# Delta-rule attention and two FFN layers: attention products with fp32 operands in place of f16 triples, and the first layer's output with tokens on rows

## The chip, the cores and the metric

The kernel runs on one core of a Trainium2 chip. The time is that of the device, in microseconds (us): the median of 3 runs, and one more execution under the profiler, which gives the trace. The engines of the core are TensorE (PE in the rows; its weight loads are PEld), VectorE (DVE), ScalarE (ACT), GpSimd (POOL) and SyncE (SP, whose queue issues nearly all DMAs).

## The reference

Attention over 4 batches, 8 heads, 768 positions and 48 features a head, then two FFN layers over all 3072 tokens:

```
for t in range(S):                       # state: 48 x 48 for each of 32 batch-heads, kept in fp32
    y[t] = q[t] @ state
    state = state + beta[t] * outer(kn[t], v[t] - kn[t] @ state)    # kn = k / (|k| + 1e-6)
x = y, as 3072 tokens x 384 features
x = leaky(x @ w1_in) @ w1_out            # 384 -> 2048 -> 384, leaky(h) = max(0.01 h, h)
x = g(x @ w2_in) @ w2_out                # 384 -> 2048 -> 384, g(h) = h - tanh(h)
```

## The kernel before

**Attention.** The sequence is cut into 12 chunks n of 64 positions; two chunks make a unit u. Within a chunk the recurrence is written with matrices: the Gram matrix of the keys (`grams`), the inverse of a unit triangular matrix (`inverses` solves its 32x32 blocks on VectorE; `merges` joins them with fp32 products of 32x32), the products of queries and keys under a causal mask (`products`), the update of the state (`states`) and the outputs (`outputs`). For every chunk there are 32 batch-heads, and a product of one head takes a quarter of TensorE's array, so four heads lie side by side. `t_batch` turns the keys: by DMA (`turn`) for chunks from 2 on, on TensorE for chunks 0 and 1.

**Numbers.** Except in `merges` and in the weights' folding, every operand is two f16 parts, a high one and the rest, and `heads` issues three products for one: high with high, high with low, low with high. VectorE and ScalarE make the parts. For queries, values and the layers' inputs they also measure a sum of squares, add it up over partitions with a product with `ones`, and scale by a power of two (`norm_sum`, `pow2_scale`, tiles `p`, `qs`, `sc`). Names in the rows: `KN` are the normalized keys in two parts, `KTp` the turned ones, `pq` queries or masked products, `XF` and `XH` the inverse (the rest and the high part), `R` the values, `S` the state and `SP` its parts.

**The FFN layers.** The tokens go in 12 tiles of 256, one for each chunk, through both layers. A layer has 8 pairs p of 128 hidden rows each way: `h_part` makes two times 9 products of 128x256 (`ps_h`), ScalarE and VectorE evict and activate (`g`, in two parts), and `o_part`, three pairs later, adds to the output (`ps_o`). Before the change the first layer holds its output with features on rows (18 products of 128x256 for a pair, `wo` stationary), the second with tokens on rows (12 products of 128x384, `g` stationary). `to_xb` evicts the first layer's output, measures it, splits it, and so makes the second layer's input.

**Weights.** `weight` builds the fp32 weights from their stored words on VectorE (rows `wi<-wo`, `wo<-wi`, 128x768 int32), then splits them: the high part on ScalarE, the rest on VectorE (`wo<-wo,sw,sx`). All of it must be done for a layer before its products start.

**The order.** `Graph` records every instruction; `schedule` places them by its own costs, by `tails` and by a table of numbers for each stage (`BIAS`), and `issue` writes them out in that order, engine by engine. All matrix products stand in the rows with line L607 (L609 after the change), and all other work with L610 (L612).

Of the kernel before, what the change touches and what calls it, by code (L numbers as in the profile page):

```python
# [30 lines left out]
def layers(n):  # L31
# [11 lines left out]
HI_DMA = ()  # L43
GQ = range(4)
# [4 lines left out]
SROOMS = 6  # L49
TURNS = 2  # L50
# [14 lines left out]
    ('dma', 'o_part1', 9): 53.93, ('dma', 'products', 1): -84.66, ('dma', 'products', 10): 73.75,  # L65
    ('dma', 'products', 11): 11.76, ('dma', 'products', 2): 87.05, ('dma', 'products', 3): -36.92,
    ('dma', 'products', 4): 60.79, ('dma', 'products', 5): 6.28, ('dma', 'products', 6): 120.47,
    ('dma', 'products', 7): 1.76, ('dma', 'products', 8): 8.32, ('dma', 'products', 9): -13.13,
    ('dma', 'queries', 0): 263.24, ('dma', 'queries', 1): 49.48, ('dma', 'queries', 10): 237.19,
    ('dma', 'queries', 11): -96.51, ('dma', 'queries', 2): -18.27, ('dma', 'queries', 3): -1.42,  # L70
    ('dma', 'queries', 4): 103.52, ('dma', 'queries', 5): 32.48, ('dma', 'queries', 6): 168.36,
    ('dma', 'queries', 7): 48.61, ('dma', 'queries', 8): 188.4, ('dma', 'queries', 9): 95.39,
    ('dma', 'to_xa', 1, 1): 43.27, ('dma', 'to_xa', 10, 1): 6.08, ('dma', 'to_xa', 11, 1): -4.4,
    ('dma', 'to_xa', 2, 1): 158.76, ('dma', 'to_xa', 3, 1): -109.25, ('dma', 'to_xa', 4, 1): 26.99,
    ('dma', 'to_xa', 5, 1): 100.67, ('dma', 'to_xa', 6, 1): 195.78, ('dma', 'to_xa', 8, 1): 20.17,
    ('dma', 'to_xa', 9, 1): 106.46, ('dma', 'v', 0): 375.3, ('dma', 'weight', 0, 0): 152.98,
    ('dma', 'weight', 0, 1): -16.73, ('dma', 'weight', 0, 2): -9.76, ('dma', 'weight', 0, 3): -81.63,
    ('dma', 'weight', 0, 4): -175.79, ('dma', 'weight', 0, 5): 3.96, ('dma', 'weight', 1, 0): 143.66,
    ('dma', 'weight', 1, 1): 108.98, ('dma', 'weight', 1, 2): 4.7, ('dma', 'weight', 1, 3): 80.95,
    ('dma', 'weight', 1, 4): 338.49, ('dma', 'weight', 1, 5): -33.2, ('dma', 'weight', 2, 0): 14.3,  # L80
    ('dma', 'weight', 2, 1): 238.2, ('dma', 'weight', 2, 2): 32.45, ('dma', 'weight', 2, 3): 11.3,
    ('dma', 'weight', 2, 4): 31.05, ('dma', 'weight', 2, 5): 94.83, ('dma', 'weight', 3, 0): 248.49,
    ('dma', 'weight', 3, 1): 141.54, ('dma', 'weight', 3, 2): -0.74, ('dma', 'weight', 3, 3): -101.97,
    ('dma', 'weight', 3, 4): 9.37, ('dma', 'weight', 3, 5): -192.26, ('first_keys', 0): 36.95,
    ('grams', 0): 41.82, ('grams', 0, 1): 47.41, ('grams', 1): 22.14, ('grams', 1, 1): 545.82,
    ('grams', 10, 1): -67.64, ('grams', 11, 1): -45.82, ('grams', 2, 1): -6.45, ('grams', 3, 1): 86.29,
    ('grams', 4, 1): -4.81, ('grams', 5, 1): -55.27, ('grams', 6, 1): 294.71, ('grams', 7, 1): -2.74,
# [6 lines left out]
    ('inverses', 0, 1): 7.54, ('inverses', 1): -33.65, ('inverses', 1, 1): 9.63, ('inverses', 2): 247.78,  # L94
    ('inverses', 2, 1): -291.34, ('inverses', 3): 28.99, ('inverses', 3, 1): -90.95, ('inverses', 4): -11.47,
    ('inverses', 4, 1): 407.53, ('inverses', 5): -6.42, ('inverses', 5, 1): 24.22, ('keys', 10): -70.46,
    ('keys', 11): 42.88, ('keys', 2): 2.73, ('keys', 3): -32.66, ('keys', 4): -249.54, ('keys', 5): -149.34,
    ('keys', 6): -33.29, ('keys', 7): -264.06, ('keys', 8): -28.32, ('keys', 9): -3.58, ('merges', 0): 61.65,
    ('merges', 0, 0): 236.37, ('merges', 0, 1): -4.82, ('merges', 1): 53.87, ('merges', 1, 1): -498.51,
    ('merges', 2): 1.17, ('merges', 2, 0): -95.98, ('merges', 2, 1): 8.62, ('merges', 3): 95.77,  # L100
    ('merges', 3, 0): -13.72, ('merges', 3, 1): -0.04, ('merges', 4): 1.69, ('merges', 4, 0): 64.24,
    ('merges', 4, 1): -40.43, ('merges', 5): -13.87, ('merges', 5, 0): -39.61, ('merges', 5, 1): 144.74,
# [124 lines left out]
class Graph:  # L227
# [116 lines left out]
    def matmul(self, o, lhsT, rhs, start, stop):  # L344
# [1201 lines left out]
```

## Time and profile before

| | |
|---|---|
| median of 3 runs | 978.83 us (977.82 to 979.18) |
| profiled execution | 976.78 us, its span 975.1 us |
| TensorE busy | 888.6 us (91%) |
| VectorE busy | 701.7 us (72%) |
| ScalarE busy | 582.0 us (60%) |
| moved by DMA | 67.01 MB, 69 GB/s mean |

The span is the time from the first to the last instruction in the trace; 1.7 us of the profiled execution lie outside it. A busy share is a mean over stages: up to the first product of the FFN layers the engines stand differently to one another than after it.

### The profile page before, as it was taken

The page shows a single profiled execution, that of the slowest core. Times are in us where ns is not written, and L with a number is a line of the kernel's source. Part 1 is how long each engine was busy: PE and PEld are TensorE (multiplying, and loading weights), DVE is VectorE, ACT ScalarE, POOL GpSimd, SP SyncE. Part 2 cuts the span into 40 slices and gives each one's busy share as a digit, 9 for nine tenths or more (in the row PEclk, how much of TensorE's full clock was granted, in tenths as well). Part 3 has the DMA queues.
Part 4 walks back from the last instruction along what each step waited for, and adds up shares of the span by engine and source line. Part 5 has one row for each costly group of instructions (what it writes and reads, how often), then busy time and mean ns, then how long its engine had stood idle before and what let it go on. Part 6 is the DMA issues. An engine that isn't in the chain of part 4 may idle for free.

```text
span 975.1 us, 35824 instructions
## 1 busy us (share of the span) xinstructions
PE 888.6 (91%) x15960; PEld 722.7 (74%) x15960; DVE 701.7 (72%) x1664; ACT 582.0 (60%) x1327; POOL 6.3 (1%) x23
## 2 busy tenths in 40 slices
PE   1236499999999999999999999999999999999997
PEld 1113488876788887788887788877788877788875
DVE  7999999999699845699873993566628957332432
ACT  6596897667786855565853645654545465444432
POOL 2000000000000000000000000000000000000000
PEclk9998599999999999999999999999999999999999
DMA  9945645222424200141020410002200000010000
GB/s 348 396 156 151 158 132 170 88 66 50 98 84 88 47 2 18 34 101 48 8 40 8 91 38 2 24 25 56 52 17 17 9 19 20 19 33 1 2 17 17
DMA packets 69274, 67.01 MB, mean 69 GB/s; under 512 B 42752, under 2 KB 54016, under 8 KB 69120
## 3 DMA queue, kind: packets, MB, share of 16 engines
q1 hardware_dynamic: 69120, 64.74, 24.3%
q8 instruction: 124, 2.03, 0.9%
q14 instruction: 30, 0.25, 0.1%
HBM read 44.14 MB, written 4.72 MB: 50 GB/s over the span
## 4 chain that ended last, share of the span: by engine, by line
PE 77%; DVE 9%; DMA 6%; ACT 5%; issue 1%; SPq 0%; ACTq 0%; DVEq 0%
PE ps_h L607 36%; PE ps_o L607 35%; PE ps_a L607 7%; DMA wo<-in_w_in_dram 3%; ACT sx L610 2%; DMA wi<-in_w_out_dram 2%; DVE sx L610 1%; DVE pq L610 1%; DVE gd L610 1%; ACT jk L610 1%; DVE wi L610 1%; DMA vf<-in_v_dram 1%; DVE xi L610 1%; DVE R L610 1%; ACT wi L610 1%
## 5 line engine op out<-in xcount | busy, mean ns | idle before, releaser
L607 PE MATMUL ps_h<-x,wi 128*128 128x256 f16 x3456 | 406.6, 273 | 0.6 <-ACT sx L610 0.4
L607 PEld LDWEIGHTS <-wi 128*128 128x128 f16 x3456 | 334.1, 98 | 47.2 <-issue 1.2
L607 PE MATMUL ps_o<-g,wo 128*128 128x256 f16 x1728 | 203.8, 273 | 0.5 <-DVE g L610 0.5
L607 PE MATMUL ps_o<-wo,g 128*128 128x384 f16 x1152 | 201.2, 326 | 0.3 <-DVE g L610 0.3
L607 PEld LDWEIGHTS <-wo 128*128 128x128 f16 x1728 | 167.1, 98 | 20.3 <-issue 0.6
L610 ACT ACTIVATE g<-sx 128x512 f16<-128x512 f32 x192 | 120.0, 627 | 83.4 <-DVE sx L610 52.8
L607 PEld LDWEIGHTS <-g 128*128 128x128 f16 x1152 | 110.5, 98 | 66.6 <-DVE g L610 0.9
L610 DVE TENSOR_TENSOR g<-sx,g 128x512 f16<-128x512 f32 x96 | 65.3, 684 | 64.4 <-ACT g L610 64.1
L610 DVE SCALAR_TENSOR_TENSOR sx<-sx,kap,ps_h 128x512 f32<-128x512 f32 x96 | 71.5, 744 | 52.1 <-ACT sx L610 51.8
L610 ACT ACTIVATE sx<-ps_h 128x512 f32<-128x512 f32 x96 | 56.4, 591 | 87.5 <-PE ps_h L607 68.9
L610 ACT ACTIVATE sx<-ps_h,kap 128x512 f32<-128x512 f32 x96 | 65.2, 680 | 59.5 <-PE ps_h L607 42.8
L610 DVE SCALAR_TENSOR_TENSOR g<-sx,g 128x512 f16<-128x512 f32 x96 | 66.0, 688 | 41.4 <-ACT g L610 41.2
L610 DVE TENSOR_TENSOR xi<-xi,gd 128x30 f32<-128x30 f32 (+9 forms) x180 | 58.9, 327 | 2.0
L610 DVE TENSOR_TENSOR gd<-xi 128x30 f32<-128x30 f32 (+9 forms) x180 | 58.8, 327 | 1.9
L607 PEld LDWEIGHTS <-KTp 48*64 48x64 f16 x3360 | 35.3, 115 | 23.1 <-issue 21.4
L610 ACT ACTIVATE jk<-kf 128x48 bf16<-128x48 f32 x160 | 38.4, 240 | 3.2
L607 PEld LDWEIGHTS <-ones 128*128 128x128 bf16 x124 | 7.6, 100 | 35.5 <-DVE svr L610 14.9
L610 ACT ACTIVATE sx<-x 128x768 bf16<-128x768 f32 x24 | 20.1, 837 | 17.3 <-DVE x L610 17.0
L610 ACT ACTIVATION_READ_ACCUMULATOR jk<-kf 128x1 f32 x160 | 30.3, 189 | 0.0
L610 DVE SCALAR_TENSOR_TENSOR wi<-wo,wi 128x768 int32<-128x768 int32 x32 | 30.0, 948 | 0.0
L610 ACT ACTIVATE sx<-x,sxs 128x768 f16<-128x768 f32 (+1 forms) x26 | 22.7, 879 | 11.5 <-DVE sxs L610 11.4
L607 PEld LDWEIGHTS <-pq 64*64 64x64 f16 (+1 forms) x2208 | 21.0, 108 | 7.8 <-issue 7.7
(151 smaller groups left out, 983.8 us busy)
## 6 DMA issues: line engine op xcount, KB each, us to landing
wo<-in_w_in_dram SPq DMA_DIRECT2D x32, 384.0 KB, 6.3
qf<-in_q_dram SPq DMA_DIRECT2D x24, 256.0 KB, 3.3
wi<-in_w_out_dram SPq DMA_DIRECT2D x14, 384.0 KB, 8.1
kf<-in_k_dram SPq DMA_DIRECT2D x12, 384.0 KB, 3.8
vf<-in_v_dram SPq DMA_DIRECT2D x12, 384.0 KB, 5.1
out_dram<-sx SPq DMA_DIRECT2D x48, 96.0 KB, 2.2
x<-in_w_out_dram SPq DMA_DIRECT2D x10, 384.0 KB, 3.9
b<-in_beta_dram SPq DMA_DIRECT2D x6, 512.0 KB, 5.7
```

The lines of the kernel that those rows point to most:

```text
L607: self.eng["pe"].matmul(out=o.real(), lhsT=lhsT.real(), rhs=rhs.real(), start=start, stop=stop)
L610: getattr(self.eng[n.on], op)(**{k: v.real() if isinstance(v, View) else v for k, v in kw.items()})
```

## The change

All products of the attention are single products with fp32 operands; `heads` and `parts` go, and with them the split of the keys' turned form, queries, masked products, inverse, values and state. Queries are only loaded (12 DMAs of 512 KB where there were 24 of 256 KB), and neither queries nor values are measured or scaled (`v_scale` goes). `t_batch` of chunks from 2 on still splits the keys (`KH`), turns both parts by DMA, and now adds them again in fp32 (`kt<-sx,sx`). The mask is applied as the product is evicted. The first layer's `o_part` is like the second's, `g` stationary, 12 products of 128x384 for a pair; `to_xb` then has tokens on rows, and the second layer's input is turned by two DMAs. `BIAS` and a few constants of the schedule are new.

```diff
-    def key_split(n, kf, y):
...
-            kn = g_.tile(s_r, [128, GM, D], F32)
-            tt(kn, kf[:, gs], y[:, gs].unsqueeze(2).to_broadcast([128, GM, D]), ALU.mult)
-            kp = [KN[n % 4][:, c_, :, g, 0:D] for c_ in range(2)]
-            copy(kp[0], kn)
-            tt(kp[1], kn, kp[0], ALU.subtract)
+    def key_norm(n, kf, y):
+        kn_t[n] = kf
+        tt(kf, kf, y.unsqueeze(2).to_broadcast([128, NM, D]), ALU.mult)
...
+            for g in range(NG):
+                copy(hi[:, :, g], kn[:, :, g])
+                tt(lo[:, :, g], kn[:, :, g], hi[:, :, g], ALU.subtract)
...
+                turn(land[c_].rearrange("p (m i) -> p m i", m=GM), KH[:, c_].rearrange("p m g d -> p (m g d)"))
+            tt(kt.rearrange("p m h i -> p (m h i)"), land[0], land[1], ALU.add)
...
-            copy(XH[:, ms], XW[:, ms])
-            tt(XF[:, ms, :, 0], XW[:, ms], XH[:, ms], ALU.subtract)
...
-        pow2_scale(qs[:, 2:3], norm_sum(ab, NG), 2 ** 14, qs[:, 3:4])
-        for g in range(NG):
-            split(q_t[n][:, g, 0], q_t[n][:, g, 1], qf[g], qs[:, 2:3])
+        q_t[n] = g_.tile(q_r, [128, NM, C], F32)
+        dma(q_t[n], q[n // 2, n % 2])
...
-            heads([(ps[g][HS[h], m], parts(kt, HD[g], m, h), parts(Q[:, h], HD[g], m)) for g, h in TILES])
+            for g, h in TILES:
+                node = mm(ps[g][HS[h], m], kt[HD[g], m, h], Q[HD[g], h * GM + m])
...
-            split(P[:, g, 0], P[:, g, 1], ps[g], 1.0 / KS)
-            pg = P[:, g].rearrange("p c m i -> p (c m) i")
-            tt(pg, pg, maskp.unsqueeze(1).to_broadcast([128, 2 * GM, C]), ALU.mult, p_engs(n))
+            stt(P[:, g * GM:(g + 1) * GM], ps[g], 1.0 / KS, maskp.unsqueeze(1).to_broadcast([128, GM, C]), ALU.mult, ALU.mult)
...
-        cp(x[:, 0:2 * N], po[0])
-        cp(x[:, 2 * N:], po[1][:, 0:N])
+        for k in range(HB2):
+            cp(rows_of(x)[:, k], po[k][:, 0:DM].rearrange("p (t f) -> p t f", t=KT))
         pow2_scale(sx[:, 1:2], squares(x), XT)
-        xb_t[n] = x_split(n + NS, x, sx[:, 1:2]), sx
+        xb_t[n] = x_turn(n, 1, x, sx[:, 1:2]), sx
...
-            for o in range(KT if i == 0 else 2):
+            for o in range(2):
...
-    ('consts', 0): 69.63, ('dma', 'b', 0): 129.4, ('dma', 'b', 1): 511.68, ('dma', 'grams', 10): 31.37,
+    ('consts', 0): -2.8, ('dma', 'b', 0): -10.37, ('dma', 'b', 1): 39.25, ('dma', 'grams', 10): 0.6,
```

VectorE, before the change, in the last stretch before the first FFN products can start. `wo_133` is the first layer's output weight, of which each row makes the rest of one pair, `KN` are keys and `XF`, `XH` the inverse in two parts:

```order
L610 SCALAR_TENSOR_TENSOR wo_133<-wo_133,sw,sx_70 128x2x384
L610 SCALAR_TENSOR_TENSOR wo_133<-wo_133,sw,sx_69 128x2x384
L610 SCALAR_TENSOR_TENSOR wo_133<-wo_133,sw,sx_65 128x2x384
L610 SCALAR_TENSOR_TENSOR wo_133<-wo_133,sw,sx_67 128x2x384
L610 TENSOR_SCALAR XF<-ps_a_93 32x8x32
L610 TENSOR_TENSOR KN_137<-sx_68,KN_137 128x8x48
L610 SCALAR_TENSOR_TENSOR wo_133<-wo_133,sw,sx_66 128x2x384
L610 TENSOR_TENSOR sx_68<-kf_75,n_109 128x384
L610 TENSOR_SCALAR wi_132<-wo_134 128x768 x2
L610 SCALAR_TENSOR_TENSOR wi_132<-wo_134,wi_132 128x768
L610 TENSOR_TENSOR XF<-XF,XH 128x1024
L610 TENSOR_SCALAR wi_132<-wo_134 128x768
```

The same stretch after the change, up to the two rows `sx_69<-x_61,sxs_113,sx_68` that make the rest of the first tile's input, which the first FFN products wait for:

```order
L612 SCALAR_TENSOR_TENSOR p_86<-ps_a_99,maskp 128x512
L612 TENSOR_SCALAR p_106<-ps_a_97 128x1
L612 SCALAR_TENSOR_TENSOR p_86<-ps_a_98,maskp 128x512
L612 TENSOR_SCALAR p_106<-p_106 128x1
L612 TENSOR_SCALAR wi_129<-wo_131 128x768
L612 TENSOR_SCALAR sxs_113<-p_106 128x1
L612 TENSOR_TENSOR gd_89<-gd_89,b_110 128x256
L612 SCALAR_TENSOR_TENSOR wi_129<-wo_131,wi_129 128x768
L612 SCALAR_TENSOR_TENSOR vf_80<-ps_a_99,vf_80 128x384
L612 SCALAR_TENSOR_TENSOR sx_69<-x_61,sxs_113,sx_68 128x384
L612 SCALAR_TENSOR_TENSOR vf_80<-ps_a_96,vf_80 128x384
L612 SCALAR_TENSOR_TENSOR sx_69<-x_61,sxs_113,sx_68 128x384
```

Here the rests of the output weight, of the inverse and the keys' split have gone from ahead of that input; the eight rows of the weight's rest stand behind it now. Counted from the start, 268 VectorE instructions stood ahead of it before, and 206 do now; the 68 that build weights from words are the same. From there to the 24th row `g<-sx,g` (an eviction of the FFN layers) VectorE has 448 instructions before and 375 after.

TensorE, in the middle of the program, the product of the inverse and the values of one chunk (`XH`, `XF` with `R`), before the change:

```order
L607 LDWEIGHTS XH
L607 MATMUL ps_a_92<-R,XH 64x48
L607 LDWEIGHTS XH
L607 MATMUL ps_a_92<-R,XH 64x48
L607 LDWEIGHTS XF
L607 MATMUL ps_a_93<-R,XF 64x48
L607 LDWEIGHTS XF
L607 MATMUL ps_a_93<-R,XF 64x48
```

And the end of the same product after it, with the first FFN product behind it:

```order
L609 MATMUL ps_a_99<-vf_79,XW 64x48 x2
L609 MATMUL ps_a_96<-vf_79,XW 64x48 x2
L609 LDWEIGHTS wi_128
L609 MATMUL ps_h_92<-x_61,wi_128 128x256
L609 LDWEIGHTS wi_128
```

Where a chunk's product took 96 pairs of a weight load and a matmul, it is 32 fp32 matmuls now. Behind the first `ps_h` there are 6816 small f16 products in the order before, and 2144 fp32 ones in the order after (1280 of 64x48, 320 of 48x48, 544 of 64x64); the 640 fp32 products of `merges` are in both. The FFN stream is interrupted by small products 105 times before and 85 times after.

## Rows read from the trace of the kernel before

**Rows 1.** Busy time by engine in four stretches: start:end, length, each engine's busy.

```profile
0.00:118.77 118.77, 42.09 (x1331) 28.75 (x1335) 110.70 (x268) 88.28 (x236) 6.25 (x23) 0.87 0.72 243
...
123.92:236.70 112.78, 112.48 (x1925) 94.72 (x1919) 108.92 (x256) 84.45 (x197) 0.00 (x0) 0.99 0.35 102
236.70:969.96 733.26, 730.21 (x12599) 596.42 (x12596) 476.40 (x1130) 404.43 (x876) 0.00 (x0) 1.00 0.16 35
969.96:975.07 5.11, 0.00 (x1) 0.00 (x0) 0.62 (x1) 0.13 (x1) 0.00 (x0) 0.75 0.32 77
```

**Rows 2.** VectorE alone from 14 us to the first tile's input.

```profile
14.00:118.77 104.77, 103.84 (x228) 0.86 0.70 233
```

**Rows 3.** All engines around the first FFN product: start, length, engine, instructions.

```profile
117.57 0.95 DVE L610 SCALAR_TENSOR_TENSOR wi<-wo,wi 128x768 int32<-128x768 int32 x1
...
118.44 0.42 DVE L610 TENSOR_SCALAR AT<-ps_a 128x256 f32<-128x256 f32 x1
...
118.77 1.14 DVE L610 SCALAR_TENSOR_TENSOR sx<-x,sxs,sx 128x384 f16<-128x384 f32 x2
...
123.92 0.61 PE L607 MATMUL ps_h<-x,wi 128*128 128x256 f16 x2
```

**Rows 4.** VectorE's groups by shape up to 118.77: count, busy, mean ns, idle.

```profile
L610 DVE SCALAR_TENSOR_TENSOR wo<-wo,sw,sx 128x768 f16<-128x768 f32 x7 | 6.8, 1008 | 0.0
L610 DVE TENSOR_TENSOR KN<-sx,KN 128x384 f16<-128x384 f32 x8 | 4.4, 547 | 0.0
L610 DVE SCALAR_TENSOR_TENSOR pq<-qf,qs,pq 128x512 f16<-128x512 f32 x4 | 3.0, 745 | 0.0
L610 DVE TENSOR_TENSOR pq<-pq,maskp 128x1024 f16<-128x1024 f16 x4 | 2.7, 681 | 0.0
L610 DVE TENSOR_TENSOR XF<-XF,XH 128x1024 f16<-128x1024 f32 x2 | 2.7, 1327 | 0.0
L610 DVE SCALAR_TENSOR_TENSOR pq<-ps_a,pq 128x512 f16<-128x512 f32 x4 | 2.6, 681 | 0.0
...
L610 DVE TENSOR_TENSOR xi<-xi,b 128x1024 f32<-128x1024 f32 x1 | 1.2, 1218 | 0.0
L610 DVE SCALAR_TENSOR_TENSOR SP<-S,sc,SP 128x384 f16<-128x384 f32 x2 | 1.2, 608 | 0.0
L610 DVE TENSOR_SCALAR p<-p 128x1 int32<-128x1 int32 x8 | 1.2, 146 | 0.0
...
L610 DVE SCALAR_TENSOR_TENSOR R<-ps_a,R 128x384 f16<-128x384 f32 x2 | 1.1, 554 | 0.2 <-ACT R L610 0.2
```

**Rows 5.** The chain that ended last, two pieces near its end.

```profile
900.42 3.93 PE ps_o L607 x36
...
926.94 3.90 PE ps_o L607 x24
```

**Rows 6.** TensorE's matmuls in order of time, two f16 product groups in a row.

```profile
545.32 0.96 PE L607 MATMUL ps_a<-SP,KTp 48*64 48x48 f16 x96
546.11 1.03 PE L607 MATMUL ps_a<-SP,pq 48*64 48x48 f16 x96
547.07 0.50 PE L607 MATMUL ps_o<-wo,g 128*128 128x384 f16 x2
```

**Rows 7.** TensorE's matmuls around one fp32 product of full size.

```profile
73.31 0.91 PE L607 MATMUL ps_a<-wi,unit_s 128*128 128x384 f32 x2 [0.35 <-ACT wi L610]
74.06 0.33 PE L607 MATMUL ps_a<-sx,unit 128*128 128x384 f16 x1
```

**Rows 8.** TensorE in the 64 fp32 products of 32x32 of one `merges` step.

```profile
358.80:359.90 1.10, 1.10 (x127) 1.09 (x128) 0.00 (x0) 0.00 (x0) 1.00 0.00 0
```

**Rows 9.** DMA turns of the layers' inputs: count, median us from issue to landing.

```profile
x<-sx SPq DMA_TRANSPOSE x22, 2.8
```

**Rows 10.** From the split of tile 2's second-layer input to its first product.

```profile
329.41 1.00 DVE L610 SCALAR_TENSOR_TENSOR x<-x,sxs,sx 128x768 f16<-128x768 f32 x1
...
330.45 0.36 DVE L610 COPY x<-sx 128x768 f16<-128x768 f16 x1
...
338.08 0.38 PE L607 MATMUL ps_h<-x,wi 128*128 128x256 f16 x2
```

More of the change, by code (lines that the diff above doesn't have):

```diff
@@ L42 @@
 LO_PE = {0: range(0, 16, 2)}
-HI_DMA = ()
-GQ = range(4)
+OUTB = range(2, 12)
+TRACE = ()
+K_SUM = ()
+GQ = range(12)
 FLIP = range(2, 12)
@@ L852, in weight @@
         acc = g_.tile(wa_r, [128, NF], F32)
-        memset(["pool"], acc, 0.0)
-        n = 2 * DM
-        c = 0
+        trace = i in TRACE
+        if trace:
+            ps = g_.tile((ps_h, ps_o)[i], [128, 512], F32)[:, 0:128]
+        else:
+            memset(["pool"], acc, 0.0)
+        c = traced = 0
         while c < NF:
@@ L875, in weight @@
         s_ = sw[:, i:i + 1]
-        pow2_scale(s_, norm_sum(acc, NF), 2 ** 15)
+        if trace:
+            diag = g_.tile(s_r, [128, 128], F32)
+            tt(diag, ps, ident, ALU.mult)
+            dve("tensor_reduce", out=acc[:, 0:1], in_=diag, axis=AX.X, op=ALU.add)
+        pow2_scale(s_, norm_sum(acc, 1 if trace else NF), 2 ** 15)
         if i in LO_PE:
@@ L919, in banks @@
         return ps
-    def heads(pairs, start=True, stop=True):
-        ab = ((0, 0), (0, 1), (1, 0))
-        for n, (a, b) in enumerate(ab):
-            for o, l, r in pairs:
-                mm(o, l[a], r[b], start and n == 0, stop and n == 2)
-    def parts(t, *ix):
-        return [t[(ix[0], c_) + ix[1:]] for c_ in range(2)]
-    def packed(t):
-        return t.rearrange("p a b c -> p (a b c)").bitcast(F32).rearrange("p (a b) -> p a b", a=t.shape[1])
-    XW = packed(XF)
     TILES = [(g, h) for g in range(NG) for h in range(2)]
-    kf_t, vf_t, b_t, x_t = {}, {}, {}, {}
-    sv_t = {}
+    kf_t, kw_t, kn_t, kt_t, vf_t, b_t, x_t = {}, {}, {}, {}, {}, {}, {}
     def load_k(n):
-        kf_t[n] = g_.tile(kf_r, [128, NM, D], F32)
+        t = g_.tile(kf_r, [128, NM * D + C - D], F32)
+        if n not in K_DMA:
+            memset(["pool"], t[:, NM * D:], 0.0)
+            kw_t[n] = t
+        kf_t[n] = t[:, 0:NM * D].rearrange("p (m d) -> p m d", m=NM)
         dma(kf_t[n], k[n // 2][:, n % 2])
@@ L1199, in states @@
             for m in range(GM):
-                heads([(ps[g][HS[h], m], parts(kt, HD[g], m, h), parts(SP, HD[g], h * GM + m)) for g, h in TILES])
-        for g in range(NG):
-            vs = vf[:, g * GM:(g + 1) * GM]
-            if not zero:
+                for g, h in TILES:
+                    mm(ps[g][HS[h], m], kt[HD[g], m, h], S[HD[g], h * GM + m])
+            for g in range(NG):
+                vs = vf[:, g * GM:(g + 1) * GM]
                 stt(vs, ps[g], -1.0 / KS, vs, ALU.mult, ALU.add)
-            copy(R[:, g, 0], vs)
-            tt(R[:, g, 1], vs, R[:, g, 0], ALU.subtract)
         g_.stage = "states", n, 1
+        U = u_t[n] = g_.tile(u_r, [128, NM, D], F32)
         m0 = s * NM
@@ L1222, in states @@
                 for m in range(GM):
-                    heads([(ps[HS[h], m], [XH[HS[h], m0 + g * GM + m], XF[HS[h], m0 + g * GM + m, :, 0]],
-                            parts(R[:, g], HS[h], m)) for h in range(2)])
-                split(R[:, g, 0], R[:, g, 1], ps, 1.0 / KS)
+                    for h in range(2):
+                        mm(ps[HS[h], m], XW[HS[h], m0 + g * GM + m], vf[HS[h], g * GM + m])
+                cp(U[:, g * GM:(g + 1) * GM], ps)
             g_.quad = True
@@ L1230, in states @@
             for m in range(GM):
[L1231 removed]
+                for g, h in TILES:
+                    mm(ps[h][HD[g], m], kn[HS[h], g * GM + m], U[HS[h], g * GM + m])
             for h in range(2):
@@ L1254, in outputs @@
                     i = h * HP + t
-                    heads([(ps[k][HS[w], i * D:i * D + D], parts(Q[:, h], HD[w ^ k], k * HP + t),
-                            parts(SP, HD[w ^ k], h * GM + k * HP + t)) for k, w in TILES])
+                    for k, w in TILES:
+                        j = h * GM + k * HP + t
+                        mm(ps[k][HS[w], i * D:i * D + D], Q[HD[w ^ k], j], S[HD[w ^ k], j])
             for k in range(HB2):
-                cp(xv[:, k], ps[k][:, 0:DM].rearrange("p (t f) -> p t f", t=KT), sc[:, 4:5])
+                src = ps[k][:, 0:DM].rearrange("p (t f) -> p t f", t=KT)
+                if after:
+                    tt(xv[:, k], src, xv[:, k], ALU.add)
+                else:
+                    cp(xv[:, k], src)
+        early = n > 0 and n not in OUTB
+        if early:
+            from_state(False)
         ps = [g_.tile(ps_a, [128, 512], F32) for h in range(2)]
```

382 lines of the change are left out of this document (174 added, 208 removed), and 27 rows, old and new, of the table BIAS.

## The prediction

> **What bounds the kernel now.** I read the busy times by stretch first, then the rows around the first FFN product, then the chain at the end. The program has three parts. Up to 118.77 us TensorE is busy only 42.09 us, while VectorE is busy 110.70 [rows 1]; from 14 us on VectorE is idle for 0.9 us in 104.77 [rows 2]. The last thing it does there is to make the rest of the first tile's input, two rows at 118.77, and TensorE turns and begins the first FFN product at 123.92, 5.15 us later [rows 3]. So that start is the sum of VectorE's work ahead of it. From 123.92 to 969.96 TensorE is busy 842.69 of 846.04 us, and the tail behind it is 5.11 us [rows 1]: there the end is the sum of TensorE's work. Between 123.92 and 236.70 both engines are nearly full (VectorE 108.92 of 112.78); later VectorE has 476.40 us of work in 733.26 and cannot set the end by its sum [rows 1]. So the change has two prices: VectorE's list ahead of the first FFN product, and TensorE's list behind it.
>
> **VectorE ahead of the first tile.** Durations are those of its shapes [rows 4]. Removed: seven rests of the output weight, which stand behind the tile now, 7 x 1.008 = 7.06; eight rests of `KN` and, taken alike, eight key normalizations of the same shape, 16 x 0.547 = 8.75; four splits of queries 2.98; four masks 2.72; four rests of the masked products 2.72; two of the inverse 2.65; two of the state 1.22; four instructions on `R`, 2.22; 22 instructions on one column (scales of queries and values), 22 x 0.146 = 3.21; two `AT` evictions at 0.42 [rows 3], 0.84. That is 67 instructions and 34.4 us. Added: four key normalizations of twice the width, by the fp32 row of 1024 columns 1.218 x 768/1024 = 0.91 each, 3.65; four rests `KH` 2.19; two sums `kt<-sx,sx` of 1024 columns, which no row shows: between the all-f16 row (0.681) and the fp32 one (1.327), I take 1.0, as the operands are f16 and the result is fp32, so 2.0, and 0.65 either way; four evictions of masked products by the row of queries, 2.98; one of `U` 0.61; three `gd` at 0.42, 1.26; two more value updates ahead, 1.11. That is 20 instructions and 13.8 us. The difference is 20.6 us of durations. An instruction holds the engine some 0.08 us less than its duration, since the row of 0.95 us at 117.57 is followed at 118.44, and the one of 0.42 by 118.77 [rows 3]; for 47 fewer that gives back 3.8, so 16.8 us. The order has 62 fewer; the other 15 are small, 15 x (0.146 - 0.08) = 1.0. Sum: **17.8 us less**, first FFN product at 106.1.
>
> Does it carry through? The seven rests now run behind that point, in the stretch in which VectorE is nearly full, 7 x 0.93 = 6.5 us. Each is needed by one pair's output products only, three pairs after its hidden products, and they stand in the order of the pairs. The stretch loses more than it is given: up to the 24th `g<-sx,g` there are 448 VectorE instructions before and 375 after. I count no further gain for that, as TensorE fills the stretch anyhow (112.48 of 112.78). DMA could take over as the limit: weights and keys keep it 0.72 busy up to 118.77 [rows 1]. The instructions that read them come up to 18 us earlier in time; I count nothing, as the words' instructions are the same 68 in both orders and stand mostly in the first half of the stretch, which is shortened least.
>
> **TensorE behind it.** *Small products.* An f16 product of the triples costs 0.79/96 = 8.2 ns (545.32 to 546.11) [rows 6]; 6816 of them are 56.1 us. An fp32 product of 384 columns took 0.75 us up to the start of the next matmul, in two passes with its first load unhidden [rows 7]: 0.977 ns a column and pass. That makes 93.8 ns for 48 columns and 125 for 64, and with four heads side by side 23.4 and 31.3. So 1600 x 23.4 + 544 x 31.3 = 54.5 us, 1.6 less. No row shows an fp32 product on a quarter of the array. Lower bound: 64 products of `merges` in 1.10 us, 17.2 ns each whatever their columns [rows 8], 36.9 us for 2144. Upper bound: only two of four heads side by side, 46.9 and 62.5 ns, 109 us. I take the middle, since the products of `merges` do run side by side: alone, 32 columns in two passes would take 62.5 ns, and they come every 17.2.
>
> *Interruptions.* From the start of a group of 96 to the next output product is 0.96 us, 0.17 more than such a group takes [rows 6]. 20 fewer interruptions (105 to 85) give 3.4 us.
>
> *Output of the first layer.* 18 products of 128x256 take half of 3.93 us, 1.965; 12 of 128x384 half of 3.90, 1.95 [rows 5]. For 96 pairs that is 1.4 us less. The sum on TensorE is **6.4 us less**.
>
> **Edits that I cost at nothing.** Fewer DMAs for queries, and ScalarE's evictions: ScalarE is busy 404.43 of 733.26 us later on [rows 1]. The turn of the second layer's input by two DMAs: such a turn lands in 2.8 us [rows 9]. Tile 2's split ends at 330.41 and its copy follows at 330.45; the first product comes at 338.08 [rows 10]. With the turns one after the other the input is there at 330.41 + 5.6 = 336.0, 2.1 us early; side by side, 4.9. The cover is the FFN work of other tiles between; without it each of 12 tiles would cost the part that is late.
>
> **Sum.** 975.1 - 17.8 - 6.4 = 950.9 of span, with 1.7 outside it 952.6 for a profiled execution. The median of the runs of before lies 2.05 above its profiled one (978.83 against 976.78); so I say 954.6.
>
> **A rule weighed against the rows.** The fp32 row has two records for one product, and 64 products of `merges` leave 127 or so [rows 7, 8]: two passes, each at twice the price of an f16 column. The Trainium skill, "FP8 and Floating Point Precision", section "TensorE Precision Notes", says that true FP32 takes four passes through the array. By records the trace does not agree (2); by time it nearly does (0.75 us is 4.6 times the 0.1625 us of an f16 product of 384 columns [rows 5]).
>
> **Rivals.**
>
> *Half of the front's gain is lost.* VectorE is no longer full because DMA, ScalarE (88.28 us busy up to 118.77) or a chain through TensorE ends last; for it speaks that three engines share the stretch, against it the 0.9 us of idle time. With 8.9 us less: 963.5.
>
> *fp32 products cost only their issue*, 17.2 ns as in `merges`: 17.6 us less than I count, 937.
>
> *Each fp32 product costs as much as four f16 ones in a row*, 4 x 8.2 = 32.9 ns whatever its columns, 70.6 us, 16.1 more: 971. Against it stand the two records and the 17.2 ns of `merges`. This is what the section named above would make of the small products.
>
> *The other side: heads do not overlap in fp32.* Of the four heads only two run side by side, because a wider operand's loads and passes shut out the other half of the array. The price is 109 us, 54.5 more than I count: 1009. It decides from (56.1 + 17.8 + 3.4 + 1.4)/2144 = 36.7 ns a product. Against it: `merges`, on smaller tiles.
>
> *The turned input is late.* If DMA turns take 4 to 5 us each behind other transfers, tiles stall 2 us each: 12 x 2 = 24, 979, and from that price on nothing is gained.
>
> **How the numbers follow.** My case 0.60 (946 to 963 by the bounds of the front, and by 20 to 27 ns a product); half of the front lost 0.15; issue price 0.08; four f16 products 0.05; two of four heads 0.07; late turns 0.05. The range that holds 8 in 10 goes from 938 to 975: it takes in the first two and the fourth, and parts of the third and last. What a measurement here can tell from no change is about 0.2%, 2 us. Faster by more: 0.60 + 0.15 + 0.08 + 0.05 and half of the last, 0.90; slower 0.08; the same 0.02.
>
> **What the profile of after would show.** Right: the first `ps_h` at 104 to 108 us with VectorE full up to then; groups of 32 fp32 products in 0.75 us (48 columns) and 1.0 us (64); 12 output products of layer one in 1.95 us; TensorE over 99% busy from the first `ps_h` on; no wait of `ps_h` for a DMA turn. Wrong: VectorE idle before 106 us for words of a weight or for TensorE; groups of 32 in over 1.2 us; idle time of TensorE put down to a transpose of `x<-sx` or to `kt<-sx,sx`.

## The result and the profile after

The changed kernel takes 966.19 us (median of 4 runs, 965.78 to 968.0), the kernel before 978.33 beside it: ratio 0.988, 95% interval 0.986 to 0.990. It is 12.1 us faster; 24.2 were forecast. The direction and the place were right, the size was half. The profiled execution took 965.78, its span 963.6, where the forecast had 950.9.

From the page of the changed kernel: busy time by engine, granted clock in 40 slices, and the chain that ended last.

```profile
PE 896.5 (93%) x12756; PEld 677.5 (70%) x12756; DVE 608.6 (63%) x1332; ACT 499.5 (52%) x1187; POOL 4.9 (1%) x22
...
PEclk9586799999999999999999999999999999999999
...
PE 79%; DVE 13%; ACT 4%; issue 2%; DMA 1%; SPq 1%; ACTq 0%; DVEq 0%
```

Busy time by stretch, to be read against [rows 1]. The cuts are the end of the first tile's input (103.27), the first FFN product (111.34), the 12th `g<-sx,g` (157.93) and the last product (958.15).

```profile
0.00:103.27 103.27, 46.26 (x1161) 33.30 (x1165) 95.78 (x211) 66.80 (x194) 4.90 (x22) 0.74 0.79 272
103.27:111.34 8.07, 7.42 (x224) 6.98 (x219) 8.07 (x16) 7.04 (x13) 0.00 (x0) 0.69 0.40 128
...
103.27:157.93 54.66, 52.17 (x588) 41.32 (x583) 53.56 (x114) 43.65 (x105) 0.00 (x0) 0.95 0.57 162
157.93:958.15 800.22, 797.76 (x11020) 602.83 (x11019) 458.61 (x1010) 388.56 (x889) 0.00 (x0) 1.00 0.19 42
```

VectorE finishes the first tile's input at 103.27, where it did so at 119.91 [rows 3]: 16.6 us earlier. From there to the first FFN product pass 8.07 us, where 4.01 did. From the first product to the start of the last, TensorE takes 846.8 us, where it took 845.7 (123.92 to 969.64). So -16.6 + 4.1 + 1.1 = -11.4 of span.

The timeline of the changed kernel around the first FFN product answers to [rows 3]; its last lines, groups of small products in the middle of the program with their weight loads (PEld), answer to [rows 6].

```profile
102.66 0.61 DVE L612 SCALAR_TENSOR_TENSOR sx<-x,sxs,sx 128x384 f16<-128x384 f32 x1
...
103.55 3.62 PE L609 MATMUL ps_a<-vf,XW 64*64 64x48 f32 x64
...
107.09 1.41 PE L609 MATMUL ps_a<-unit,sx 128*128 128x128 f16 x12
...
108.45 1.15 PE L609 MATMUL ps_a<-u,p 64*64 64x48 f32 x64
...
110.25 1.16 PE L609 MATMUL ps_a<-q,kt 48*64 48x64 f32 x64 [0.65 <-ACT x L612]
...
111.34 1.37 PE L609 MATMUL ps_h<-x,wi 128*128 128x256 f16 x11
...
116.50 1.14 PE L609 MATMUL ps_h<-x,wi 128*128 128x256 f16 x9 [1.05 <-ACT sx L612]
...
549.97 1.02 PEld L609 LDWEIGHTS ps_a<-u,p 64*64 64x64 f32 x64 [0.32 <-issue]
...
549.98 1.15 PE L609 MATMUL ps_a<-u,p 64*64 64x48 f32 x64
551.05 2.14 PE L609 MATMUL ps_h<-x,wi 128*128 128x256 f16 x18
...
578.79 0.94 PE L609 MATMUL ps_a<-u,kf 64*48 64x48 f32 x64
579.66 6.07 PE L609 MATMUL ps_h<-x,wi 128*128 128x256 f16 x54
```

Behind the input three groups of 32 fp32 products run before the first FFN product, one of them, `vf,XW`, at half clock (granted 0.50 up to 108 us) and on two quarters of the array: 3.5 us until the input's own turn (`ps_a<-unit,sx`) starts. Before the change the turn began while the input was being made, and only products of `KTp` stood behind it:

```profile
119.00 2.01 PE L607 MATMUL ps_a<-unit,sx 128*128 128x128 f16 x12
...
120.94 0.71 PE L607 MATMUL ps_a<-KTp 48*64 48x64 f16 x26
...
122.82 1.17 PE L607 MATMUL ps_a<-KTp 48*64 48x64 f16 x70 [1.17 <-issue]
```

Later in the changed kernel, a group of 32 products with 64 stationary columns takes 1.07 us up to the next matmul, one with 48 takes 0.87. Each product leaves two records of a matmul and two of a weight load; in the group at 549.98 the 64 loads take 1.02 of the 1.07 us.

### The profile page after: what moved, and what is told of

Read it like the earlier page. It is cut to its first block, busy times and chain, and to the rows that moved or that the text cites. A ratio compares the mean times of both kernels' runs of the same rounds, so it can differ in the third digit from the quotient of the medians.

```text
span 963.6 us, 29002 instructions
## 1 busy us (share of the span) xinstructions
PE 896.5 (93%) x12756; PEld 677.5 (70%) x12756; DVE 608.6 (63%) x1332; ACT 499.5 (52%) x1187; POOL 4.9 (1%) x22
## 4 chain that ended last, share of the span: by engine, by line
PE 79%; DVE 13%; ACT 4%; issue 2%; DMA 1%; SPq 1%; ACTq 0%; DVEq 0%
PE ps_h L609 36%; PE ps_o L609 35%; PE ps_a L609 8%; DVE xi L612 3%; DVE wo L612 3%; DVE wi L612 3%; DVE gd L612 2%; ACT gd L612 1%; DVE g L612 1%; DMA wo<-in_w_in_dram 1%; ACT sx L612 1%; DVE sx L612 1%; ACT XW L612 1%; ACT jk L612 1%; ACT wo L612 1%
## 5 line engine op out<-in xcount | busy, mean ns | idle before, releaser
L609 PE MATMUL ps_o<-wo,g 128*128 128x384 f16 x2304 | 400.9, 326 | 0.2 <-issue 0.2
L609 PEld LDWEIGHTS <-g 128*128 128x128 f16 x2304 | 221.9, 98 | 132.9 <-issue 0.5
L609 PE MATMUL ps_a<-q,kt 48*64 48x64 f32 x768 | 15.1, 229 | 13.8 <-DMA q<-in_q_dram 11.4
L612 DVE SCALAR_TENSOR_TENSOR sx<-x,sxs,sx 128x768 f16<-128x768 f32 (+1 forms) x26 | 24.6, 951 | 4.6 <-ACT sx L612 4.4
L612 ACT ACTIVATE gd<-ps_a 32x256 f32<-32x256 f32 (+1 forms) x72 | 23.9, 373 | 5.2 <-PE ps_a L609 4.6
L609 PEld LDWEIGHTS ps_a<-q,kt 48*64 48x64 f32 x768 | 13.3, 142 | 16.6 <-ACT wo L612 11.5
L612 DVE TENSOR_SCALAR sx<-ps_o,kap 128x384 f32<-128x384 f32 x12 | 7.4, 618 | 27.5 <-PE ps_o L609 25.5
```

Of the source, the lines that this page charges most:

```text
L609: self.eng["pe"].matmul(out=o.real(), lhsT=lhsT.real(), rhs=rhs.real(), start=start, stop=stop)
L612: getattr(self.eng[n.on], op)(**{k: v.real() if isinstance(v, View) else v for k, v in kw.items()})
```

## Experiments

A and B name the two sides of each question anew. Times are medians, ratios those to the kernel before, with their intervals. "Path" is the time from the first FFN product's start to the last product's (846.8 in the changed kernel).

### What sets the price of a small fp32 product

**e1_stat48**: fewer stationary columns where a product has 64 stationary and 48 moving.

```
+ if lhsT.ap.dtype == F32 and n.stage[0] == "outputs" and n.stage[1] >= 2 and tuple(lhsT.shape)[1] == 64 and tuple(rhs.shape)[1] == 48:
+     o, lhsT = o[0:48], lhsT[:, 0:48]
```

> The changed kernel with its order untouched; in the outputs of chunks 2 to 11 the 640 fp32 products of 64x48 load only 48 of their 64 stationary columns (the last 16 positions of each chunk's output are left out). Theory A, the price of such a product is its two weight loads, so it goes by the stationary columns: 29.5 ns a product in the changed kernel fall to the 23.2 ns of the 48x48 products, 640 x 6.3 = 4.0 us less, 962 us. Rival B, the price is that of the moving columns in two passes (48 in both): no change, 966 us.

962.3 us (0.984, 0.982 to 0.986), path 842.6. TensorE's timeline of this kernel at the same groups, with the loads of `u,p`:

```profile
541.07 1.10 PE L611 MATMUL ps_a<-vf,XW 64*64 64x48 f32 x64
542.10 3.12 PE L611 MATMUL ps_h<-x,wi 128*128 128x256 f16 x27
...
547.10 0.81 PEld L611 LDWEIGHTS ps_a<-u,p 64*48 64x48 f32 x64 [0.32 <-issue]
...
547.11 0.94 PE L611 MATMUL ps_a<-u,p 64*48 64x48 f32 x64
547.97 2.14 PE L611 MATMUL ps_h<-x,wi 128*128 128x256 f16 x18
```

`u,p` with 48 stationary columns fell from 1.07 to 0.86 and its loads from 1.02 to 0.81; `vf,XW`, left at 64, takes 1.03. The 4.2 us off the path are ten groups each of `u,p` and `S,q` at 0.21.

**e2_mov24**: the other operand, half its columns in all products of 64x48.

```
+ if lhsT.ap.dtype == F32 and n.stage[1] >= 2 and tuple(lhsT.shape)[1] == 64 and tuple(rhs.shape)[1] == 48:
+     o, rhs = o[:, 0:24], rhs[:, 0:24]
```

> The changed kernel with its order untouched; all 1280 fp32 products of 64x48 of chunks 2 to 11 move only 24 of their 48 columns (half of each product is left out). Theory A, weight loads of 64 columns set the price: 29.5 ns stay, 966 us. Rival B, the passes of the moving columns set it: the price halves or falls to the 17.2 ns of the 32x32 products, 1280 x 12 to 15 ns = 16 to 19 us less, 947 to 950 us.

965.31 us (0.986, 0.985 to 0.988), path 846.3. TensorE's timeline:

```profile
549.98 1.02 PEld L611 LDWEIGHTS ps_a<-u,p 64*64 64x64 f32 x64 [0.32 <-issue]
...
549.98 1.13 PE L611 MATMUL ps_a<-u,p 64*64 64x24 f32 x64
551.04 2.14 PE L611 MATMUL ps_h<-x,wi 128*128 128x256 f16 x18
```

Half the moving columns leave the group at 1.06 us. So the price goes by the stationary columns and not by the moving ones, and the loads, which fill the group in all three kernels but for 0.04 to 0.05 us, set it where 64 columns are stationary and 48 or fewer pass. With four heads side by side a head's next product comes after four products, 4 x 29.5 = 118 ns with two loads: 59 ns a load of 64 columns; 4 x 23.2 = 93, 46 a load, for 48. The Trainium skill, "TensorE: Matmul & The Clock Gate", section "LDWEIGHTS (loading the stationary operand)", gives a load's time as its columns divided by 1.2, an estimate of 53 and 40 ns: the trace agrees on the step (13 ns for 16 columns) and is 6 ns above on each. The Trainium skill, "FP8 and Floating Point Precision", section "TensorE Precision Notes", gives true fp32 four passes; this run cannot tell two from four, since half the columns change the time by a hundredth and the passes, however many, lie behind the loads.

**e5_cut**: one f16 product of 128x128 in the middle of 40 groups of 64x48, to price an interruption.

```
+ if j == 16 and lhsT.ap.dtype == F32 and n.stage[1] >= 2 and tuple(lhsT.shape)[1] == 64 and tuple(rhs.shape)[1] == 48:
+     bank = o.buf.ring.rooms[o.buf.slot][:, 384:512]
+     self.eng["pe"].matmul(out=bank, lhsT=self.ident.real(), rhs=self.ident.real(), start=True, stop=True)
```

> The changed kernel with its order untouched; in the middle of each of the 40 groups of fp32 products of 64x48 of chunks 2 to 11 stands one f16 product of 128x128 on the full array, into columns of the bank that nobody reads. Theory A, each change between the full array and quarters of it costs some 0.08 us on the way in and 0.12 on the way out, so each cut costs 0.20 and the product 0.06: 40 x 0.26 = 10.4 us more, 976.6 us. Rival B, only the added product counts: 40 x 0.06 = 2.4 us, 968.6 us.

978.39 us (1.001, 1.000 to 1.002), path 859.3: 12.5 / 40 = 0.31 us a cut. TensorE's timeline of one group:

```profile
549.50 0.63 PE L612 MATMUL ps_a<-vf,XW 64*64 64x48 f32 x32
550.06 0.23 PE L611 MATMUL ps_a<-unit 128*128 128x128 f16 x1
550.22 0.68 PE L612 MATMUL ps_a<-vf,XW 64*64 64x48 f32 x32
550.84 3.12 PE L612 MATMUL ps_h<-x,wi 128*128 128x256 f16 x27
```

1.34 us instead of 1.03, and the product itself is worth 0.05 (a third of the 0.163 of a 384-column one). Going from fp32 quarters to the whole array and back costs a quarter of a microsecond. No run cut a group of f16 products in the same way.

**e6_o256**: the first layer's output products as 18 of 128x256 again.

```
+ if i == 0:
+     node.calls["pe"] = [(po[o // 2][:, o % 2 * N:o % 2 * N + N], WO[0][:, f, 1 - a, o * 128:(o + 1) * 128], gj[:, b],
+                          ...
```

> The changed kernel with its order untouched; the first layer's output products have the shape of the kernel before again, 18 of 128x256 for a pair instead of 12 of 128x384 (the values that reach the second layer are then not the layer's output, and two products are added to fill a bank). Theory A, a pair takes 1.965 us instead of 1.95: 96 x 0.015 + 0.2 = 1.6 us more, 968 us. Rival B, more weight loads and changes of form cost more than their sum, or evictions now end last: 3 us or more.

966.87 us (0.989, 0.987 to 0.991), path 848.5: 1.7 us more on the path, near the 1.6 expected. But the path lies between 845.1 and 848.1 in four runs that keep every product as it is (e3_turn, e8_dve, e9_flip1, e13_act), and the time is within what can be told apart: the small price is not shown, a price of 3 us or more is out.

### Whether VectorE's list sets the end, ahead of the first FFN product and behind it

**e8_dve**: the sums `kt<-sx,sx` of chunks 2 and 3 four times, 6.8 us more ahead of the input. **e10_dve2**: a transposition of the inverse four times, 6.1 us more right behind it.

```
+ again = 4 if n.on == "dve" and n.stage in (("grams", 2), ("grams", 3)) and op == "tensor_tensor" and kw["out"].shape[-1] == 1024 else 1
+ for _ in range(again - 1):
...
+ if n.stage == ("inverses", 1) and op == "transpose" and kw["out"].buf.ring.name == "xi":
+     for _ in range(3):
```

> The changed kernel; VectorE makes the sums of the turned keys of chunks 2 and 3 four times each instead of once (the same result), six more rows of 1.14 us of VectorE's time, 6.8 us, ahead of tile 0's input. Theory A, VectorE's list sets when that input is there: the rest of the input and the first ps_h come 6.5 to 7 us later (first ps_h at 118), and the time rises by as much, 973 us. Rival B, TensorE's fp32 products at half clock or DMA set the front: the first ps_h moves by under 3 us, at most 969 us.

> The changed kernel with its order untouched; VectorE makes the first transposition of unit 1's inverse four times instead of once (the same result), 3 more rows of 2.05 us, 6.1 us, right behind the rest of tile 0's input, where they no longer delay that input. Theory A, VectorE's list goes on to set the time behind the first ps_h, up to some 213 us: the time rises by 5 to 6 us as it did for work put ahead of the input, 971 to 972 us, with ps_h idle for weights or evictions between 111 and 213 us. Rival B, from the first ps_h on TensorE's list is the bound and VectorE only has to keep up: its idle time of some 2 to 6 us in this stretch takes most of it, 966 to 969 us.

e8_dve: 973.61 us (0.995, 0.993 to 0.996), +7.4; first FFN product at 118.34, first `g<-sx,g` at 125.41, both 7 later. e10_dve2: 972.87 (0.995, 0.993 to 0.997), +6.7. Its timeline:

```profile
106.65 6.33 DVE L614 STREAM_TRANSPOSE xi<-gd 128x1024 f32<-128x1024 f32 x3
...
111.15 4.10 PE L609 MATMUL ps_h<-x,wi 128*128 128x256 f16 x36
...
122.28 2.08 PE L609 MATMUL ps_h<-x,wi 128*128 128x256 f16 x9 [7.02 <-ACT sx L615]
```

Here the first FFN product stays at 111.15, TensorE does 36 hidden products, and then stands for 7.02 us until the first of them are evicted. The time grows nearly as much as in e8_dve. Two stretches of this run, from the input's end to the 12th `g<-sx,g` and around the wait:

```profile
102.95:165.04 62.09, 55.07 (x588) 43.40 (x582) 60.08 (x116) 44.05 (x105) 0.00 (x0) 0.89 0.49 140
120.50:127.30 6.80, 5.02 (x25) 3.55 (x25) 6.80 (x12) 5.14 (x9) 0.00 (x0) 0.50 0.63 194
```

While TensorE stood, the granted clock fell to 0.50, and the nine hidden products behind the wait took 2.08 us where they take 1.14 in the changed kernel; so the clock is mixed into the 6.7 us. VectorE's own rows show what set the pace: up to the 12th `g<-sx,g` it is busy 6.5 us longer than in the changed kernel (60.08 against 53.56), and idle only 0.9 us longer. Where the first product starts decides nothing by itself: work added to VectorE's list counts one to one on both sides of it.

### Whether another order takes the hand-over back

**e4_front** moves the input's turn, its evictions and 36 hidden products ahead of chunk 1's `vf,XW`; **e3_turn** only the turn and its evictions.

```
+ first = [late[i] for i in (555, 556, 532, 533, 535, 536, 534, 537, 538, 1734, 1735, 1739, 1740)]
+ order = [n for n in order if n not in first]
+ at = order.index(late[547])
+ order[at:at] = first
```

(e3_turn has the first nine numbers.)

> The changed kernel; on TensorE the turn of tile 0's input and the first 36 hidden products now stand ahead of chunk 1's product of inverse and values, its outputs and chunk 2's product of queries and keys (96 fp32 products), and the evictions that go with them stand ahead too; nothing else moves. Theory A, these products at half clock stand between VectorE's last work on the input and the first FFN product: the first ps_h comes at 105.5 to 106.5 us instead of 111.3, and since the 96 products then run later at full clock, 3 to 4 us are gained in all, 962 to 963 us. Rival B, the first FFN product waits for something else (an eviction on ScalarE, words of a weight): it comes at 109 us or later, and under 1.5 us are gained.

> The changed kernel; only the turn of tile 0's input on TensorE (12 products and the evictions that go with it) stands ahead of chunk 1's product of inverse and values; the hidden products stay behind all of it. Theory A, from 103.8 us on TensorE is full of work and the 4 us between VectorE's last work on the input and the first ps_h are products, not a wait: the turn begins at 104.3 us, but the first ps_h still comes at 110.5 to 111.5 us and the time is the same, 965 to 967 us. Rival B, the turned input's eviction is what the first ps_h waits for: it comes at 108 us and 3 us are gained, 963 us.

e4_front: 970.94 us (0.992, 0.990 to 0.994), 4.7 slower than the changed kernel, although its first FFN product starts at 105.69. Its timeline:

```profile
105.69 5.63 PE L609 MATMUL ps_h<-x,wi 128*128 128x256 f16 x36
...
111.25 2.07 PE L609 MATMUL ps_a<-vf,XW 64*64 64x48 f32 x64
...
113.78 1.02 DVE L612 SCALAR_TENSOR_TENSOR wo<-wo,sw,sx 128x768 f16<-128x768 f32 x1 [4.33 <-ACT sx L612]
...
122.34 2.08 PE L609 MATMUL ps_h<-x,wi 128*128 128x256 f16 x9 [6.08 <-ACT sx L612]
```

ScalarE's next work is the eviction of `vf,XW`, which is now late; behind it VectorE stands for 4.33 us, and TensorE gives back more than it had won. Up to the 12th `g<-sx,g` VectorE has no more work than in the changed kernel (53.92 us busy, 53.56 there), but it is idle 6.7 us instead of 1.1. And with TensorE's own wait of 6.08 us the granted clock stands at 0.50 from 118.9 to 125.7: the nine hidden products at 122.34 take 2.08 us, not 1.14. e3_turn: 967.6 (0.989, 0.987 to 0.992), first product at 112.82: no gain either. Its granted clock stayed at 0.50 until 115 us, and `u,p` took 1.84 us instead of 1.15.

**e9_flip1**: `vf,XW` of chunk 1 on four quarters.

```
- mm(ps[HS[h], m], XW[HS[h], m0 + g * GM + m], vf[HS[h], g * GM + m])
+ mm(ps[HS[h ^ (g if n == 1 else 0)], m], XW[HS[h], m0 + g * GM + m], vf[HS[h], g * GM + m])
...
```

Behind "..." the two halves are issued in turn, and one eviction becomes two of 64 rows.

> The changed kernel; chunk 1's product of inverse and values, 32 fp32 products that stand ahead of the first ps_h on two quarters of the array at a time (104 ns each at half clock), lies on all four quarters as in the later chunks; one eviction of 128 rows becomes two of 64 rows. Theory A, these products are on the path and take 1.9 us instead of 3.3: the first ps_h comes 1.2 to 1.5 us earlier, at 110, and the time falls by as much, 964.8 us. Rival B, VectorE's list ends last in this stretch: the time stays within 0.5 us of 966.2.

966.79 us (0.989, 0.987 to 0.991). The product is shorter, but TensorE waits for ScalarE three times, once in it and twice behind it (0.77, 0.57, 1.02 us), the clock stays at 0.50 until 114, and the first FFN product comes at 114.09. No gain.

**e11_gfirst** and **e12_evict**: the turn and 18 hidden products ahead of `vf,XW`, and evictions of the first pairs ahead of other work: in e11_gfirst on VectorE, in e12_evict on ScalarE too, ahead of the parts of the output weight. The first two lines are in both runs, the last two in e12_evict.

```
+ move((555, 556, 532, 533, 535, 536, 534, 537, 538, 1734, 1735), 547, 0)
+ move((1739, 1740), 549, 1)
...
+ move((216, 207, 1741, 1742, 1743), 209, 0)
+ move((558, 559, 560, 561, 743, 744), 228, 1)
```

> The changed kernel; on TensorE the turn of tile 0's input and 18 hidden products stand ahead of chunk 1's product of inverse and values and 18 more behind it, and on VectorE the first row g<-sx,g stands ahead of the four additions of chunk 1's outputs and the two masked products that wait for the moved products. All else is as it was. Theory A, what carries into the rest of the time is when VectorE comes to its first g<-sx,g, not when the first ps_h starts: that row moves from 118.1 to 115.5 us, the first ps_h to 106, and the time falls by 2 to 3 us, 963.5 to 964.5 us. Rival B, TensorE's list from 103.8 us on is full anyway and these products only change places: the time stays within 0.8 us of 966.2.

> The changed kernel with the moves on TensorE of the run before this one (turn of tile 0's input and 18 hidden products ahead of chunk 1's product of inverse and values, 18 behind it); now on ScalarE and VectorE the evictions of the first two hidden pairs stand ahead of most of the parts of the output weight, and the additions and masked products of the attention behind them. Theory A, the parts of the output weight, which the change put between tile 0's input and the first evictions on ScalarE and VectorE, are what TensorE waits for behind the first ps_h: with the evictions ahead of them the first g<-sx,g comes at 110 us, the waits of 4.3 and 1.3 us seen in that run are gone, and the time falls to 963 to 965 us. Rival B, VectorE's whole list up to some 213 us is what ends last, in whatever order: the time stays at 966 to 968 us, with the waits further behind.

e11_gfirst: 971.15 us (0.994, 0.992 to 0.995). Eight high parts of the weight stand ahead of the first eviction on ScalarE (it comes at 118.13), so the first `g<-sx,g` is at 119.40, not earlier. e12_evict: 968.79 (0.990, 0.988 to 0.992), 2.6 slower on the median, with an interval that overlaps that of the changed kernel. Its timeline:

```profile
110.03 0.69 DVE L612 TENSOR_TENSOR g<-sx,g 128x512 f16<-128x512 f32 x1
...
121.11 0.16 PE L609 MATMUL ps_a<-ab,ones 128*128 128x1 bf16 x1 [5.23 <-ACT sx L612]
```

The first `g<-sx,g` is now 8 us earlier, and TensorE still stands for 5.23 us a little later; the 12th is at 162.10, 4.2 us later than in the changed kernel. In both runs the granted clock fell to 0.50 in these waits, as in e4_front: it stood there from 116.6 to 126.9 in e11_gfirst, where TensorE had a wait of 4.29 us, and from 117.7 to 124.6 in e12_evict. TensorE did 6.80 and 3.48 us of work in these stretches (3.36 in that of e4_front); if half of it is the clock's, an estimate, that is 3.4 and 1.7 us. So the three orders lost by waits and by the clock that fell in them, and no run parts the two.

**e13_act**: eight evictions from VectorE to ScalarE, 3.4 us.

```
+ for n in order:
+     if n.idx in (500, 512, 661, 516, 517, 1805, 1806, 1881):
+         n.on = "act"
```

> The changed kernel with its order untouched; eight evictions that VectorE makes before 190 us (three of the state and values of chunks 0 and 1, two of the inverse and the Gram matrix, three of the first layer's output of tiles 0 and 1) are made by ScalarE instead, which has gaps of 1 to 8 us there. They occupy VectorE for 3.4 us. Theory A, up to some 213 us VectorE's list is what carries into the time, whatever the order: VectorE comes to its twelfth g<-sx,g some 1.9 us earlier (five of the eight lie ahead of it), and the time falls by 1.5 to 3 us, 963.2 to 964.7 us. Rival B, TensorE's list is the bound from the first products on, or ScalarE takes the place of VectorE: the time stays within 0.7 us of 966.2 or rises.

966.0 us (0.987, 0.985 to 0.989): nothing gained. Its timeline, ahead of the input:

```profile
98.37 0.69 DVE L612 SCALAR_TENSOR_TENSOR p<-ps_a,maskp 128x512 f32<-128x512 f32 x1 [2.48 <-PE ps_a L609]
```

Five of the eight evictions lie ahead of the input. VectorE is busy 2.0 us less up to it (93.76 against 95.78), but stands for 2.48 here, and the input is done at 103.50, no earlier than in the changed kernel (103.27). So near this point VectorE's sum, and a chain through TensorE and ScalarE that it is part of, end within a few us of each other: more work on VectorE shows in full, less does not.

## Why the prediction was half right

**VectorE ahead of the first tile: right.** 16.6 us less against 17.8. Of the 1.2 missing, 0.4 are the two sums `kt<-sx,sx`, and 0.4 is idle time of VectorE from 14 us on (1.38 us, where it was 0.93). VectorE's groups by shape in the changed kernel, three that the change adds, up to 104 us, and behind the last "..." one from the stretch behind it:

```profile
L612 DVE SCALAR_TENSOR_TENSOR p<-ps_a,maskp 128x512 f32<-128x512 f32 x4 | 2.7, 678 | 0.0
...
L612 DVE TENSOR_TENSOR kt<-sx,sx 128x1024 f32<-128x1024 f16 x2 | 2.4, 1218 | 0.0
L612 DVE TENSOR_TENSOR KH<-kf,KH 128x384 f16<-128x384 f32 x4 | 2.2, 548 | 0.0
...
L612 DVE SCALAR_TENSOR_TENSOR wo<-wo,sw,sx 128x768 f16<-128x768 f32 x8 | 8.2, 1020 | 0.0
```

The sums took 1.218 us each, the fp32 price of [rows 4], where I took 1.0; the other two came out within 0.07 us of their rows. The last row is from the stretch behind the input, 103.27 to 157.93.

**"Does it carry through?" was the step that failed in front.** It held the 5.15 us from VectorE's last rows to the first FFN product as they were, and counted the seven rests of the output weight at nothing, because "the stretch loses more than it is given" and "as TensorE fills the stretch anyhow". The hand-over grew by 4.06 us, with the products that the new order put between input and turn. And the stretch is VectorE's at least as much as TensorE's: from the input's end to the 12th `g<-sx,g` VectorE is busy 53.56 us of 54.66, TensorE 52.17. The same stretch before:

```profile
119.91:172.99 53.08, 51.84 (x900) 45.44 (x899) 50.80 (x120) 46.25 (x135) 0.00 (x0) 0.94 0.53 150
```

So it did not lose work, it gained 2.8 us of it, in 114 rows where there were 120. The 448 and 375 instructions by which the forecast judged it reach too far: they count to the 24th `g<-sx,g` of the first layer alone, which in the traces is at 312.16 us before and 287.46 after, when VectorE has long had time to spare ([rows 1], from 236.70 on). The 24th row of that name in either layer is at 227.11 and 212.70, with 242 instructions from the input on before and 238 after. Eight rests of the output weight are in the stretch to the 12th row now (8.2 us), one was before (1.0); what else left the stretch made up for part of that. The rests were not taken off VectorE's path, they were put behind a point that sets nothing by itself. So the 16.6 us won at the input are 15.1 at the 12th `g<-sx,g` (172.99 to 157.93), and e10_dve2 shows that work added to VectorE in this stretch counts in full. That taking the rests out of it would give their 8.2 us back is not shown: no run did that, and e13_act, which took other rows off VectorE, gained nothing. The forecast had 106.1 for the first FFN product and TensorE's savings on top from there on; a sum of VectorE's list up to that later row would have kept the rests in it.

That the hand-over alone is to blame is not what the runs show: e4_front, e11_gfirst and e12_evict bring the first FFN product to 105.5 to 105.7, near the 106.1 of the forecast, and none is faster: two are slower by 4.7 and 5.0 us, e12_evict by 2.6, which is not clear of the noise. From the 12th `g<-sx,g` to the last product's start 800.2 us pass in the changed kernel, and 799.0 to 801.2 in the eight runs that leave the products as they are; before the change it was 796.65 (172.99 to 969.64).

**"Small products" on TensorE: one price was mis-sized.** The sum of passes gave 23.4 ns for 64x48 and 48x48 alike and 31.3 for 64x64. From start to start, over all records behind the first `ps_h`, they are 29.5 for the four products with 64 stationary and 48 moving columns, 23.2 for `u,kf` with 48, and 30.3 for 64x64. 1280 x 6.1 = 7.8 us too little; against it stand 0.5 at 64x64 and 2.5 because the f16 triples cost 8.6 ns on the mean rather than 8.2. So the small products grew by 3.1 us instead of shrinking by 1.6. The passes of [rows 7], from a product of 384 columns, cannot show a load that is longer than the passes; e1_stat48 and e2_mov24 show that the price goes with the stationary columns, and the rows of the loads that these fill the time.

**"Interruptions" gave nothing.** Entering and leaving small products cost 16.8 us over 105 interruptions before (the time of the last product ahead and the last small one, start to start, above what such products usually take), and 17.0 over 85 after: 0.16 each became 0.20. Fewer by 20, and dearer by a quarter. e5_cut, at 0.25 and the product itself, shows that changing over from fp32 quarters costs; that it costs more than with f16 rests on the two means, and what of it is the load or the end of the products before, no run tells.

**Sum.** Span forecast 950.9, measured 963.6. The 12.7 are 1.2 (VectorE up to the input), 4.1 (hand-over) and 7.5 (TensorE behind it: 4.7 in the small products, 3.6 in the interruptions, 0.8 back in output products, `merges` and `ones`). Cut at the 12th `g<-sx,g`, which VectorE sets, they are 2.7 in front (15.1 of the 17.8) and 10.0 behind it, where the time grew by 3.6 us instead of falling by 6.4 (between the first FFN product and that row 2.5 us less pass than before, so part of the longer hand-over was made up there).

**The rest held.** Output products gave 2.0 us (1.4 forecast). Turns of the second layer's input land in 2.8 us on the median, as in [rows 9], and no FFN product waits for one: that rival is out. So is "two of four heads" (46.9 ns at the least; 29.5 came). "Four f16 products in a row", 32.9 ns whatever the columns, is out by the 23.2 of `u,kf`, though the 29.5 of the others lies between it and my 23.4. "Issue price" is out above 32x32. "Half of the front's gain is lost" came near in amount (963.5), but that is luck: VectorE was full up to the input, a small part of the gain was lost behind it, and the rest of the shortfall is TensorE's.

**Open:** what bounds VectorE, ScalarE and TensorE together at 95 to 125 us once VectorE has less to do (e13_act); and an order that beats the changed kernel was not found: of the twelve runs only e1_stat48, which leaves out work, was faster by more than can be told apart.

## What to carry to other kernels

When an engine is full on both sides of a milestone, count its list up to the point from which it has time to spare, not up to the milestone; work moved past the milestone is not saved, and a count of rows that runs past that point says nothing. Such a sum prices added work; relief is worth less where another chain ends close behind (e13_act). Price a small fp32 product by its weight loads as well as by its passes, and take each change between quarters and the whole array as a price of its own. Before an order is changed by hand, look at every engine's next row: in e4_front and e11_gfirst three engines that wait for one another gave an early start back within a few rows, and the granted clock fell while TensorE stood.

## What the runs showed of the hardware that was not expected

- Two fp32 loads a product, 59 ns for 64 stationary columns and 46 for 48, set the pace with four quarters in use, whether 24 or 48 columns pass.
- One whole-array product between fp32 quarters costs 0.31 us, some six times its own time (0.05, an estimate from a product of 384 columns).
- A VectorE sum of f16 operands with an fp32 result takes the fp32 time: 1.218 us for 1024 columns, where the all-f16 product took 0.681 [rows 4].
- TensorE's granted clock fell to 0.50 while it stood waiting for evictions in the four runs with its longest waits behind the first FFN product: 7.02 us in e10_dve2 (0.50 from 120.5 to 127.3), 6.08 in e4_front, 5.23 in e12_evict, 4.29 in e11_gfirst. In the changed kernel, where it waited 1.05 us at most, the clock stayed at full there.
- Behind the same groups of products on TensorE the granted clock came back from 0.50 at 108.3 us in the changed kernel and between 107.4 and 110.3 in e1_stat48, e2_mov24, e5_cut, e6_o256 and e10_dve2; in e3_turn and e9_flip1, which change the order or the quarters there, only at 115.2 and 114.1. Why it came late is open, and so is what it cost: `u,p` took 1.84 us in e3_turn instead of 1.15, but 1.96 in e6_o256 too, where the first FFN product came at 111.17, no later than in the changed kernel.
